# A linear-attention and channel-mix kernel: nine token slots per partition, two-row-group matmuls, and every engine in a fixed planned order

## The chip, the cores and the metric

One core of a Trainium2 chip runs the whole kernel. The metric is device time in microseconds (us), the median over executions. The core has five engines with a queue each: TensorE (PE in the profile, its weight loads PEld), VectorE (DVE), ScalarE (ACT), GpSimd (POOL) and SyncE (SP). DMAs are issued from POOL (those that also change the type from f32 to bf16) and from SP.

## The reference

For 8 batches, 8 heads, 576 tokens and head size 64:

```
proj = x @ w_phi                       # 64 -> 128, for x = q and x = k
proj = proj - max|proj| over features  # one number per token
phi  = [exp(proj), exp(-proj)]         # 256 features
kv = k_p^T v ; z = sum of k_p          # per head, over 576 tokens
attn = (q_p kv) / (q_p z + 1e-6)
x = attn, heads side by side           # (8, 576, 512)
xk, xr = token mixes of x and x one token earlier
out = sigmoid(xr @ w_r) * (relu(xk @ w_k)^2 @ w_v)   # 512 -> 1024 -> 512
```

Note that the maximum is subtracted before both exponentials: exp(p - m) and exp(-(p - m)).

## The kernel before, in words

**Pairs.** `attention_pair` (L144) handles two heads of one batch; there are 32 pairs. Head h keeps tokens 4p to 4p+3 on partition p (512 tokens), and the last 64 tokens of the two heads share one extra 128-partition group, the tail. DMA transposes (L137, SP) turn `nat` (tokens on partitions) into `qkT` (the 64 features of two token groups stacked on 128 partitions). One projection matmul multiplies such a block by `wboth`, two copies of w_phi on the diagonal of a 128x256 matrix of which half is zero.

**The k maximum** is not subtracted in the projection. DVE takes max|proj| (L161, L163), ACT makes exp(-m) and exp(+m) (`em`, L171, L172), and POOL multiplies v by them into `v12` (L178, L181), two versions of v that kv (L231) reads. **The q maximum** is transposed through TensorE (`mhl`, L197 to L200, copied out at L202) and added to the transposed q projection by small matmuls with the selector `sel` (L212).

**The mix and the channel mix.** `mix` (L274) builds xk and xr for a whole batch on DVE (L284 to L295) after its four pairs. `moe` (L298) runs 32 matmuls for h (L304), ReLU on ACT (L307), a square on POOL (L308), 16 matmuls for r (L313), 32 for v (L319), and a last DVE step (L322). Tails of two batches are joined into one smaller `moe` call.

**Order.** Python issues the four pairs of batch b and then the channel mix of batch b-1 (L336 to L349). The framework's scheduler orders each engine's queue by itself and weaves the two. PSUM has 8 banks: tag P (2 buffers of 2 banks: ps_k, ps_q, ps_qT), tag B (2 of 1 bank), tag mo (2 of 1 bank). Each engine runs its queue in order: an instruction that waits holds up what stands behind it.

Of the kernel before, what the change touches and what calls it, by code (L numbers as in the profile page):

```python
# [8 lines left out]
FP = mybir.dt.float32  # L9
# [3 lines left out]
AX = mybir.AxisListType  # L13


@with_exitstack
def kernel(
# [15 lines left out]

    nc = tc.nc
# [6 lines left out]
    SM = 512  # L41
    TAIL = S - SM
    NDC = DM // 128
    NFC = FF // 128
    NG = 9 * NP
    XW = 128 + S
# [3 lines left out]
    mid = ctx.enter_context(tc.tile_pool(name="mid", bufs=3))  # L50
    small = ctx.enter_context(tc.tile_pool(name="small", bufs=4))
    xpool = ctx.enter_context(tc.tile_pool(name="xpool", bufs=2))
# [15 lines left out]
    nc.gpsimd.tensor_copy(ident, ident_f32)

    sel2 = consts.tile([128, 9], FP, name="sel2")  # L70
    nc.vector.tensor_tensor(sel2, ident_f32[:, 0:9], ident_f32[:, 9:18], op=ALU.add)
    sel = consts.tile([128, 9, 128], BF, name="sel")
    nc.vector.tensor_copy(sel, sel2.to_broadcast([128, 9, 128]))
    hmask = consts.tile([128, 2], FP, name="hmask")
    nc.vector.memset(hmask, 0.0)
    nc.vector.memset(hmask[0:64, 0:1], 1.0)
    nc.vector.memset(hmask[64:128, 1:2], 1.0)

    NMH = 3
    mhls = []  # L80
    for i in range(NMH):
        t = consts.tile([128, 128], BF, name=f"mhl{i}")
        nc.vector.memset(t, 0.0)
        mhls.append(t)
    NVT = 2
    vts = []
    for i in range(NVT):
        t = consts.tile([128, H, 5, D], FP, name=f"vt{i}")
        nc.gpsimd.memset(t[:, :, 4, :], 0.0)
        vts.append(t)  # L90

# [6 lines left out]
    def load_weights():  # L98
        nc.sync.dma_start(out=mu_k_t, in_=moe_mu_k.rearrange("(c p) -> p c", p=128))
        nc.sync.dma_start(out=mu_r_t, in_=moe_mu_r.rearrange("(c p) -> p c", p=128))  # L100
        nc.gpsimd.dma_start(out=wk_bf, in_=moe_w_k.rearrange("(c p) f -> p c f", p=128))
        nc.gpsimd.dma_start(out=wr_bf, in_=moe_w_r.rearrange("(c p) f -> p c f", p=128))
        nc.gpsimd.dma_start(out=wv_bf, in_=moe_w_v.rearrange("(c p) f -> p c f", p=128))
        nc.vector.tensor_scalar(wv_bf, wv_bf, 0.5, None, op0=ALU.mult)

    def load(b, parts):
        nat = inp.tile([128, NG, 128], BF, name="nat")
        qkT = inp.tile([128, NG, 128], BF, name="qkT")  # L110
        vt = vts[b % NVT]
        flat = nat.rearrange("p g c -> p (g c)")
        flatT = qkT
        tails = flat[:, 32 * 128:].rearrange("p (a t d) -> p a t d", a=NP, t=2)
        for (a0, a1) in parts:
            hs = slice(2 * a0, 2 * a1)
            for (src, base) in ((k, 16), (q, 0)):
                nc.gpsimd.dma_start(
                    out=flat[:, (base + 4 * a0) * 128:(base + 4 * a1) * 128].rearrange(
                        "p (h x) -> p h x", x=256),  # L120
                    in_=src[b, hs, 0:SM, :].rearrange("h (p j) d -> p h (j d)", j=4))
            for (src, t) in ((k, 1), (q, 0)):
                for hh in range(2):
                    nc.gpsimd.dma_start(  # L124
                        out=tails[64 * hh:64 * hh + 64, a0:a1, t, :],
                        in_=src[b, 2 * a0 + hh:2 * a1:2, SM:S, :].rearrange("a i d -> i a d"))
            nc.sync.dma_start(
                out=vt[:, hs, 0:4, :].rearrange("p h j d -> p h (j d)"),
                in_=v[b, hs, 0:SM, :].rearrange("h (p j) d -> p h (j d)", j=4))
            for hh in range(2):  # L130
                nc.sync.dma_start(
                    out=vt[64 * hh:64 * hh + 64, 2 * a0 + hh:2 * a1:2, 4, :],
                    in_=v[b, 2 * a0 + hh:2 * a1:2, SM:S, :].rearrange("a i d -> i a d"))
            rng = [(0, NG)] if (a0, a1) == (0, NP) else [
                (16 + 4 * a0, 16 + 4 * a1), (4 * a0, 4 * a1), (32 + a0, 32 + a1)]
            for (g0, g1) in rng:
                nc.sync.dma_start_transpose(out=flatT[:, g0:g1, :],  # L137
                                            in_=flat[:, g0 * 128:g1 * 128])
        return qkT, vt

    xs_of = {}
    pair_no = [0]

    def attention_pair(b, hp, qkT, vt):  # L144
        n = pair_no[0]
        pair_no[0] += 1
        xs = xs_of[b]
        gq, gk, gt = 4 * hp, 16 + 4 * hp, 32 + hp


        ps_k = psum.tile([128, 8, 128], FP, name="ps_k", tag="P", bufs=2)
        for g in range(4):
            nc.tensor.matmul(ps_k[:, 2 * g:2 * g + 2, :].rearrange("p c f -> p (c f)"),  # L153
                             lhsT=qkT[:, gk + g, :], rhs=wboth,
                             start=(g % 2 == 0), stop=(g % 2 == 1))

        ps_t = psum.tile([128, 4, 128], FP, name="ps_t", tag="B", bufs=2)
        nc.tensor.matmul(ps_t[:, 0:2, :].rearrange("p c f -> p (c f)"),
                         lhsT=qkT[:, gt, :], rhs=wboth, start=True, stop=True)
# [12 lines left out]
        nc.scalar.activation(em[:, 1, :], mkf, AF.Exp)  # L172
        emt = em.rearrange("p a (h j) -> p a h j", h=2)[:, :, :, 4]
# [206 lines left out]
```

## Time and profile before

| | |
|---|---|
| median of 2 runs | 507.23 us (506.62 to 507.83) |
| the profiled execution, its own time | 509.07 us |
| its span in the trace | 507.3 us |
| mean granted TensorE clock | 0.942 |
| DMA traffic | 40.92 MB |

The span is what the trace covers from the first to the last instruction. Busy time is the time in which an engine executes; matmul ends are modelled. "Idle before" is time for which an engine stood still just before an instruction, with the one that released it.

### The profile page before, as it was taken

What the parts mean: (1) busy time and instruction counts of PE and PEld (TensorE: products, weight loads), DVE (VectorE), ACT (ScalarE), POOL (GpSimd) and SP (SyncE); (2) the same over time, 40 slices, a digit from 0 to 9 for tenths busy, and PEclk for the clock granted to TensorE, in tenths of its full rate; (3) what the DMA queues carried; (4) which work ended last, traced back from release to release, by engine and by line L of the source; (5) the groups of instructions that cost most, each with busy time, mean ns of one, the idle gap of its engine ahead of it and who ended that gap; (6) DMA issues with size and microseconds to landing.
All of it is one profiled execution on the core that took longest, in us unless ns stands there. A gap on an engine that the chain in (4) does not pass through costs nothing.

```text
span 507.3 us, 7519 instructions
## 1 busy us (share of the span) xinstructions
PE 336.2 (66%) x2832; PEld 194.5 (38%) x2832; DVE 296.2 (58%) x615; ACT 213.2 (42%) x389; POOL 247.1 (49%) x374
## 2 busy tenths in 40 slices
PE   0131434566875868877875688768857887888695
PEld 0011223343443434544443445435434554445232
DVE  1031403467845795686568755875567659874921
ACT  1020313243643454556444554476344734753232
POOL 8534152246643465377327753574237426662342
PEclk9999999999898799989997899899958998889899
DMA  9999980178018800990149404600460011001012
GB/s 153 181 196 191 143 95 0 60 128 95 0 43 229 94 1 21 209 156 1 43 129 150 45 22 146 124 3 22 129 121 0 22 43 43 1 1 63 21 42 63
DMA packets 84515, 40.92 MB, mean 81 GB/s; under 512 B 53120, under 2 KB 79360, under 8 KB 84480
## 3 DMA queue, kind: packets, MB, share of 16 engines
q1 hardware_dynamic: 56752, 28.39, 24.2%
q0 software_dynamic: 27728, 12.06, 19.9%
q8 instruction: 22, 0.36, 0.3%
q14 instruction: 13, 0.11, 0.1%
HBM read 33.62 MB, written 9.44 MB: 85 GB/s over the span
## 4 chain that ended last, share of the span: by engine, by line
PE 31%; POOL 30%; DVE 18%; DMA 10%; issue 7%; ACT 4%; POOLq 0%; DVEq 0%; ACTq 0%
POOL v L178 15%; PE ps_v L319 6%; POOL kk L308 6%; DMA nat<-in_q_dram 5%; PE ps_h L304 5%; DMA qkT<-nat 4%; PE ps_kv L231 4%; PE ps_r L313 3%; DVE xr L290 3%; PE ps_nd L249 3%; DVE mk L161 2%; PE ps_k L153 2%; DVE tr L293 2%; POOL nat L124 2%; DVE x_sc L260 2%
## 5 line engine op out<-in xcount | busy, mean ns | idle before, releaser
L308 POOL TENSOR_TENSOR kk<-krelu 128x512 bf16<-128x512 bf16 (+1 forms) x96 | 85.1, 904 | 90.7 <-ACT krelu L307 90.2
L178 POOL TENSOR_TENSOR v<-vt,em 128x640 bf16<-128x640 f32 x64 | 82.6, 1314 | 1.1
L304 PE MATMUL ps_h<-xk,wk_bf 128*128 128x512 bf16 x256 | 77.2, 420 | 6.6 <-DVE xk L290 4.9
L319 PE MATMUL ps_v<-wv_bf,kk 128*128 128x512 bf16 x288 | 75.5, 379 | 1.4 <-POOL kk L308 1.4
L307 ACT ACTIVATE krelu<-ps_h 128x512 bf16<-128x512 f32 (+1 forms) x96 | 46.2, 497 | 70.8 <-PE ps_h L304 61.6
L223 ACT ACTIVATE q_p<-ps_qT 128x1024 bf16<-128x1024 f32 x32 | 32.8, 1026 | 97.1 <-PE ps_qT L212 97.0
L185 ACT ACTIVATE k_p<-ps_k 128x1024 bf16<-128x1024 f32 x32 | 32.8, 1024 | 66.7 <-DVE mk L161 66.7
L231 PE MATMUL ps_kv<-v,k_p 128*128 128x65 bf16 x256 | 16.4, 209 | 58.4 <-POOL v L181 55.9
L161 DVE TENSOR_REDUCE mk<-ps_k 128x8 f32<-128x1024 f32 x32 | 39.1, 1221 | 24.6 <-PE ps_k L153 24.4
L236 DVE CAST kv<-ps_kv 128x260 bf16<-128x260 f32 x32 | 13.7, 427 | 60.7 <-PE ps_kv L233 60.6
L197 POOL CAST mhl<-nm 128x9 bf16<-128x9 f32 x32 | 9.5, 298 | 78.7 <-DVE nm L166 78.7
L304 PEld LDWEIGHTS <-wk_bf 128*128 128x128 bf16 x384 | 34.8, 103 | 33.7 <-issue 14.5
L194 DVE TENSOR_REDUCE nm<-ps_q 128x8 f32<-128x1024 f32 x32 | 39.0, 1218 | 14.2 <-PE ps_q L191 14.1
L322 DVE SCALAR_TENSOR_TENSOR ob<-rt,ps_v 128x512 f32<-128x512 bf16 x36 | 24.7, 686 | 30.2 <-PE ps_v L319 18.4
L316 ACT ACTIVATE rt<-ps_r 128x512 bf16<-128x512 f32 x36 | 21.7, 602 | 44.4 <-PE ps_r L313 43.9
L153 PE MATMUL ps_k<-wph,qkT 128*128 128x256 bf16 x128 | 23.8, 306 | 23.9 <-DMA qkT<-nat 22.5
L207 PE MATMUL ps_qT<-qkT,wph 128*128 128x512 bf16 x64 | 29.3, 458 | 11.2 <-DVE nm L194 10.4
L319 PEld LDWEIGHTS <-kk 128*128 128x128 bf16 x288 | 26.4, 98 | 25.1 <-POOL kk L308 2.6
L313 PE MATMUL ps_r<-wr_bf,xr 128*128 128x512 bf16 x128 | 35.6, 379 | 0.0
L290 DVE SCALAR_TENSOR_TENSOR xr<-diff,mu_r_t,xs 128x512 bf16<-128x512 bf16 x32 | 34.8, 1088 | 0.0
L224 ACT ACTIVATE q_n<-ps_qT 128x1024 bf16<-128x1024 f32 x32 | 33.4, 1044 | 0.0
L191 PE MATMUL ps_q<-wph,qkT 128*128 128x256 bf16 x128 | 26.7, 320 | 9.6 <-ACT k_n L186 9.1
(81 smaller groups left out, 696.7 us busy)
## 6 DMA issues: line engine op xcount, KB each, us to landing
out_dram<-ob SPq DMA_DIRECT2D x32, 256.0 KB, 2.4
vt<-in_v_dram SPq DMA_DIRECT2D x7, 1024.0 KB, 6.5
nat<-in_k_dram POOLq DMA_DIRECT2D x7, 512.0 KB, 6.4
nat<-in_q_dram POOLq DMA_DIRECT2D x7, 512.0 KB, 8.9
vt<-in_v_dram SPq DMA_DIRECT2D x4, 256.0 KB, 4.7
wk_bf<-in_moe_w_k_dram POOLq DMA_DIRECT2D x1, 1024.0 KB, 9.0
wv_bf<-in_moe_w_v_dram POOLq DMA_DIRECT2D x1, 1024.0 KB, 17.6
out_dram<-ob SPq DMA_DIRECT2D x8, 128.0 KB, 2.7
```

What stands on the lines that cost most here:

```text
L153: nc.tensor.matmul(ps_k[:, 2 * g:2 * g + 2, :].rearrange("p c f -> p (c f)"), lhsT=qkT[:, gk + g, :], rhs=wboth, start=(g % 2 == 0), stop= ...
L161: nc.vector.tensor_reduce(mk[:, :, 0:4], ps_k.rearrange("p (h j) f -> p h j f", h=2), axis=AX.X, op=ALU.max, apply_absolute_value=True)
L178: nc.gpsimd.tensor_tensor(v12[:, pn, :, 0:64], vp.rearrange("p (s d) -> p s d", d=D), em[:, pn, :].to_broadcast([128, 10, D]), op=ALU.mult)
L194: nc.vector.tensor_reduce(nm[:, 0:8], ps_q, axis=AX.X, op=ALU.max, apply_absolute_value=True, negate=True)
L224: nc.scalar.activation(q_n, qT8, AF.Exp, scale=-1.0)
L231: nc.tensor.matmul(ps_kv[:, pn, h, :], lhsT=kx[:, c, :], rhs=v12[:, pn, 5 * h + j, :], start=(pn == 0 and c == 0), stop=False)
L290: nc.vector.scalar_tensor_tensor(out=xo[:, c, :], in0=diff[:, c, 0:SM], scalar=mu[:, c:c + 1], in1=xs[:, c, 0:512], op0=ALU.mult, op1=ALU.add)
L304: nc.tensor.matmul(ps_h[:, 0:w], lhsT=wk_bf[:, c, fc * 128:(fc + 1) * 128], rhs=xk[:, c, :], start=(c == 0), stop=(c == NDC - 1))
L307: nc.scalar.activation(krelu[:, 0:w], ps_h[:, 0:w], AF.Relu)
L308: nc.gpsimd.tensor_tensor(kk[:, fc, 0:w], krelu[:, 0:w], krelu[:, 0:w], op=ALU.mult)
L313: nc.tensor.matmul(ps_r, lhsT=xr[:, c, cs], rhs=wr_bf[:, c, :], start=(c == 0), stop=(c == NDC - 1))
L319: nc.tensor.matmul(ps_v, lhsT=kk[:, fc, cs], rhs=wv_bf[:, fc, :], start=(fc == 0), stop=(fc == NFC - 1))
```

## The change

It rewrites the kernel's body.

- **Layout.** Token = 9p + s with 64 partitions per head; two heads fill 128 partitions, nine slots s each, no tail tokens. Per pair k has slots 0 to 8 and q slots 0 to 8, which give nine transposed blocks: four of k, four of q, and one ("edge") that holds slot 8 of k on rows 0 to 63 and slot 0 of q on rows 64 to 127. One edge block per pair is handled for four pairs at once (`add_edge`). Loads are one DMA each for k, q and v per batch (batch 0 in three parts).
- **Row-tiled matmuls.** Projections, maximum adds and kv use 64 of the 128 rows of the array per matmul, in pairs on rows 0 to 63 and 64 to 127 that write different PSUM banks. The zero halves of `wboth` go.
- **The k maximum** goes the way of the q maximum: both are negated, transposed together, and `ka` adds the k one to the finished projection in PSUM. v is only cast to bf16 (`vc`); exp(m), exp(-m) and `v12` go.
- **Moved work.** The kv copy goes from DVE to ACT. The mix is made per pair (`df`, `xa`, `xb`). The two divisions per pair become one pass of 640 columns.
- **PSUM.** Tag P has 3 buffers of 2 banks, mo 2 of 1 bank, B goes.
- **Order.** Every step is registered with an engine, a cost, a due time (one pair each T = 8.2) and the buffers that it takes and frees; `Plan.order` places them greedily, the engine that can start soonest first, and the code is emitted in that order under a manual schedule. In the plan a `nat` buffer counts as free when SP has issued the transposes that read it (cost 0.6 on SP), and the next load into it stands on POOL from then on; on the chip that load waits for the transposes themselves.

```diff
+LAG = {"PE": 0.25, "ACT": 0.2, "DVE": 0.15, "POOL": 0.2, "SP": 0.05, "DMA": 1.8}
+SWITCH = 0.12
+    def order(self, bufs, loose=()):
...
+                if e == "PE":
+                    cands = [(t + (SWITCH if o["mode"] != self.mode else 0.0), o) for (t, o) in cands]
+                t0 = min(c[0] for c in cands)
+                pick = min((c for c in cands if c[0] <= t0 + 0.12),
+                           key=lambda c: (c[1]["due"], c[1]["idx"]))
+                if best is None or pick[0] < best[0]:
+                    best = pick
...
+        op(f"lk{tag}", "POOL", 0.7, due, ld(0), alloc=al("nat"), chain="lk")
+        op(f"lq{tag}", "POOL", 0.7, due, ld(1), [f"lk{tag}"])
+        op(f"tr{tag}", "SP", 0.6, due, tr, [f"lk{tag}.d", f"lq{tag}.d"], alloc=al("qkT"),
+           rel=[("nat", b)])
+        op(f"tr{tag}.d", "DMA", 1.5 * n, due, None, [f"tr{tag}"])
...
+    for i, (nm_, dst, src, g) in enumerate((("wk", wk_bf, moe_w_k, 6.5), ("wr", wr_bf, moe_w_r, 3.2),
+                                            ("wv", wv_bf, moe_w_v, 6.5))):
+        op(nm_, "POOL", 0.7, i - 8, ldw(dst, src), ["tr1.0"])
...
+        def proj(tag, gg):
+            ps = ptile(("P", tag + N), "ps_" + tag)
+            for g in range(4):
+                for par in range(2):
+                    r = slice(64 * par, 64 * par + 64)
+                    nc.tensor.matmul(ps[:, par, g * 128:(g + 1) * 128],
+                                     lhsT=qkT[b][r, g0 + gg + g, :], rhs=wph[r, :],
+                                     start=(g == 0), stop=(g == 3))
...
+        def ka():
+            for par in range(2):
+                r = slice(64 * par, 64 * par + 64)
+                nc.tensor.matmul(s["k"][:, par, :], lhsT=s["mT"][r, :],
+                                 rhs=sel[r, 0:4, :].rearrange("p g f -> p (g f)"),
+                                 start=False, stop=True, skip_group_check=True)
...
+        def kv():
+            s["kvp"] = ps = ptile(("P", "kv" + N), "ps_kv")
+            for pn in range(2):
+                for c in range(8):
+                    par, g = divmod(c, 4)
+                    for hh in range(2):
+                        r = slice(64 * hh, 64 * hh + 64)
+                        nc.tensor.matmul(ps[:, hh, pn * 65:(pn + 1) * 65], lhsT=s[f"k{pn}"][r, c, :],
+                                         rhs=vb[r, a, 2 * g + par, :],
+                                         start=(pn == 0 and c == 0), stop=False)
...
+        op("qp" + N, "PE", 0.25, d0, qp, [f"tr{pt}.d", "dve1"], alloc=[("P", ("P", "q" + N))], chain="qp",
+           mode=1, rel=[("qkT", b)])
...
+        op("mh" + N, "POOL", 0.5, d0 + 2, mhx, ["rk" + N, "dve2"], alloc=al("mhl"), rel=[("nm", n)],
+           chain="mh")
+        op("mt" + N, "PE", 0.06, d0 + 2.2, mt, ["mh" + N, "dve3"], rel=[("mhl", n)],
...
+        op("kv" + N, "PE", 0.65, d0 + 6, kv, ["eb" + N, "vc" + N, f"ekt{pt}"],
...
+        op("kc" + N, "ACT", 0.4, d0 + 6.5, kvc, ["kv" + N], rel=[("P", "kv" + N)], alloc=al("kvs"),
```

Per pair the steps are, in this order of need: `qp`, `kp` (projections, 8 matmuls of 128 columns each), `rq`, `rk` (maxima, DVE), `mh` (POOL), `mt` (transpose), `mc` (DVE), `ka` (2 matmuls of 512), `qt` (2 of 512 and 8 of 128), `ea`, `eb`, `qa`, `qb` (exponentials of 1024 columns, ACT), `kv` (36 matmuls of 65), `kc`, `nd` (18, full array), `rd` (DVE), `xt` (5 transposes), `xe`, `df`, `xa`, `xb` (DVE). The channel mix keeps its matmuls, with 128 edge tokens from each two batches (`add_moe_edge`).

## Rows read from the trace of the kernel before

**Rows 1.** The page, busy time of each engine: us, share of the span, instructions.

```profile
PE 336.2 (66%) x2832; PEld 194.5 (38%) x2832; DVE 296.2 (58%) x615; ACT 213.2 (42%) x389; POOL 247.1 (49%) x374
```

**Rows 2.** Windows: from:to, length, busy us (instructions) of each engine, clock, DMA share, GB/s.

```profile
20.00:40.00 20.00, 5.32 (x19) 2.48 (x20) 5.52 (x6) 4.18 (x6) 8.03 (x13) 1.00 1.28 188
40.00:60.00 20.00, 7.28 (x62) 5.20 (x62) 5.72 (x14) 4.74 (x8) 7.09 (x10) 1.00 1.46 180
...
212.00:264.00 52.00, 40.84 (x368) 23.47 (x366) 35.41 (x71) 28.76 (x54) 29.05 (x46) 0.97 0.43 85
...
368.00:420.00 52.00, 39.17 (x353) 23.52 (x353) 34.53 (x76) 26.20 (x49) 24.06 (x36) 0.87 0.21 49
```

**Rows 3.** Chain that ended last, 200 to 264 us: start, us, engine, tile, line.

```profile
208.04 8.00 DMA qkT<-nat
...
236.07 2.48 POOL v L178 x2
...
246.94 2.44 POOL v L178 x2
```

**Rows 4.** Waits: who waited for whom, total us, times, longest us.

```profile
PE ps_kv L231 <- POOL v L181: 55.9, 26, 13.3
...
POOL nat L118 <- DMA qkT<-nat: 25.0, 4, 11.9
```

**Rows 5.** Chain, 200 to 264 us: TensorE groups at full clock, us and count.

```profile
205.63 0.26 PE ps_kv L231 x8
...
206.59 0.52 PE ps_nd L249 x16
...
250.30 0.22 PE ps_qT L212 x4
...
250.83 0.22 PE ps_qT L207
251.04 0.86 PE ps_r L313 x4
```

**Rows 6.** Timeline, TensorE: start, duration, of one nd matmul.

```profile
155.19 0.19 PE L249 MATMUL ps_nd<-kv,q_n 128*128 128x65 bf16 x1
```

**Rows 7.** Lines, shapes apart: busy us, mean ns, idle before and its releaser.

```profile
L178 POOL TENSOR_TENSOR v<-vt,em 128x640 bf16<-128x640 f32 x64 | 82.6, 1314 | 1.1
L308 POOL TENSOR_TENSOR kk<-krelu 128x512 bf16<-128x512 bf16 x64 | 70.9, 1123 | 68.7 <-ACT krelu L307 68.5
L161 DVE TENSOR_REDUCE mk<-ps_k 128x8 f32<-128x1024 f32 x32 | 39.1, 1221 | 24.6 <-PE ps_k L153 24.4
L307 ACT ACTIVATE krelu<-ps_h 128x512 bf16<-128x512 f32 x64 | 37.6, 607 | 56.9 <-PE ps_h L304 52.8 <-POOL kk L308 3.9
L290 DVE SCALAR_TENSOR_TENSOR xr<-diff,mu_r_t,xs 128x512 bf16<-128x512 bf16 x32 | 34.8, 1088 | 0.0
L223 ACT ACTIVATE q_p<-ps_qT 128x1024 bf16<-128x1024 f32 x32 | 32.8, 1026 | 97.1 <-PE ps_qT L212 97.0
L260 DVE TENSOR_TENSOR x_sc<-ps_nd,rden 128x320 bf16<-128x320 f32 x64 | 31.1, 488 | 1.4
L322 DVE SCALAR_TENSOR_TENSOR ob<-rt,ps_v 128x512 f32<-128x512 bf16 x36 | 24.7, 686 | 30.2 <-PE ps_v L319 18.4 <-issue 7.7 <-ACT t_n L221 3.5
L267 DVE COPY xs<-ps_x 128x512 bf16<-128x512 bf16 x32 | 13.4, 419 | 3.4 <-PE ps_x L265 3.3
```

**Rows 8.** Timeline, VectorE: one mix step with POOL idle beside it.

```profile
228.20 0.74 DVE L290 SCALAR_TENSOR_TENSOR xr<-diff,mu_r_t,xs 128x512 bf16<-128x512 bf16 x1
```

**Rows 9.** Windows around one long stop of TensorE, columns as in rows 2.

```profile
158.00:161.00 3.00, 0.10 (x1) 0.10 (x1) 3.00 (x5) 1.78 (x4) 0.71 (x3) 1.00 1.25 242
...
164.00:167.00 3.00, 2.29 (x20) 1.75 (x20) 1.74 (x4) 0.00 (x0) 2.14 (x6) 0.50 0.02 5
```

**Rows 10.** Chain, the end of the kernel: start, us, what.

```profile
472.03 0.49 DVE diff L285
...
478.31 9.71 POOL kk L308 x8
```

More of the change, by code (lines that the diff above doesn't have):

```diff
@@ L63 @@
-    wboth = wph.rearrange("p a f -> p (a f)")
+    BUFS = {"P": 3, "mo": 2, "nat": 2, "qkT": 2, "vt": 2, "v1": 2,
+            "kpn": 2, "qpn": 2, "tl": 2, "xk": 2, "kk": 2, "krelu": 3, "rt": 3, "ob": 3,
+            "xs": 2, "mhl": 3, "mk": 3, "nm": 3, "mT": 3, "kvs": 2, "x": 2, "me": 2, "d": 2, "mTe": 2}
+    T = 8.2
+    plan = Plan()
+    op = plan.op
+    wph_f32 = consts.tile([128, F], FP, name="wph_f32")
+    wph = consts.tile([128, F], BF, name="wph")
     ident_f32 = consts.tile([128, 128], FP, name="ident_f32")
-    make_identity(nc, ident_f32)
@@ L67 @@
     ident = consts.tile([128, 128], BF, name="ident")
[L68 to L90, printed above, removed]
+    sel3 = consts.tile([128, 3, 8], FP, name="sel3")
+    sel = consts.tile([128, 8, 128], BF, name="sel")
+    mhls = [consts.tile([128, 128], BF, name=f"mhl{i}") for i in range(BUFS["mhl"])]
@@ new lines, with get, heads @@
+    op("wphi", "SP", 1.2, -60, c_wphi)
+    op("wphi.d", "DMA", 0.1, -60, None, ["wphi"])
+    op("ident", "POOL", 1.5, -49.5, c_ident)
+    op("dve1", "DVE", 0.2, -9, c_dve1, ["wphi.d"])
+    op("dve2", "DVE", 0.6, -8, c_dve2)
+    op("dve3", "DVE", 0.8, -7, c_dve3, ["ident"])
+    nat, qkT, vt = {}, {}, {}
+    def get(dct, key, pool, shape, dtype, name, **kw):
+        if key not in dct:
+            dct[key] = pool.tile(shape, dtype, name=name, **kw)
+        return dct[key]
+    def heads(src, b, a0, a1):
+        return src[b, 2 * a0:2 * a1].rearrange("h (p s) d -> (h p) (s d)", s=R).rearrange(
+            "(a r) x -> r a x", r=128)
@@ new lines, in add_load, with ld, f, ldv @@
+    def add_load(b, a0, a1, due, first):
+        al = lambda t: [(t, (t, b))] if first else []
+        n = a1 - a0
+        tag = f"{b}.{a0}"
+        def ld(which):
+            def f():
+                t = get(nat, b, inp, [128, NP, 2 * X], BF, "nat")
+                src, o = ((k, 0), (q, X))[which]
+                nc.gpsimd.dma_start(out=t[:, a0:a1, o:o + X], in_=heads(src, b, a0, a1))
+            return f
+        def ldv():
+            t = get(vt, b, inp, [128, NP, X], FP, "vt")
+            nc.sync.dma_start(out=t[:, a0:a1, :], in_=heads(v, b, a0, a1))
+        def tr():
+            t = get(qkT, b, inp, [128, NP * R, 128], BF, "qkT")
+            nc.sync.dma_start_transpose(out=t[:, R * a0:R * a1, :],
+                                        in_=nat[b][:, a0:a1, :].rearrange("p a x -> p (a x)"))
+        g = 1.0 * n
+        op(f"lk{tag}", "POOL", 0.7, due, ld(0), alloc=al("nat"), chain="lk")
+        op(f"lk{tag}.d", "DMA", g, due, None, [f"lk{tag}"])
+        op(f"lq{tag}", "POOL", 0.7, due, ld(1), [f"lk{tag}"])
+        op(f"lq{tag}.d", "DMA", g, due, None, [f"lq{tag}"])
+        op(f"tr{tag}", "SP", 0.6, due, tr, [f"lk{tag}.d", f"lq{tag}.d"], alloc=al("qkT"),
+           rel=[("nat", b)])
+        op(f"tr{tag}.d", "DMA", 1.5 * n, due, None, [f"tr{tag}"])
+        op(f"lv{tag}", "SP", 0.6, due + 0.1, ldv, alloc=al("vt"), chain="lv")
+        op(f"lv{tag}.d", "DMA", g, due + 0.1, None, [f"lv{tag}"])
@@ L353 @@
+    BUFS["kke"] = 1
+    for b in range(B):
+        add_moe(b)
+        if b % 2 == 1:
+            add_moe_edge(b // 2)
+    seq = plan.order(BUFS, ("P", "mo"))
+    with tc.manual_schedule():
+        for o in seq:
+            if o["fn"] is not None:
+                o["fn"]()
 _INS = ['q', 'k', 'v', 'w_phi', 'moe_mu_k', 'moe_mu_r', 'moe_w_k', 'moe_w_v', 'moe_w_r']
```

754 lines of the change are left out of this document (521 added, 233 removed).

## The prediction

> **What bounds the kernel now.** I read the busy times first. No engine is busy for more than 66% of the span [rows 1], so no single engine sets the time. In a steady stretch of 52 us TensorE works 41 of them and VectorE 35 [rows 2]: about 13 us pass per pair. Next the chain of waits: it goes through POOL's two passes over v in every pair, 2.48 us at 236.07 and 2.44 us at 246.94 [rows 3]. The waits show why: kv waited for these passes 26 times, 55.9 us in all [rows 4]. So the kernel runs at the length of a chain, in which POOL's multiplication of v stands between the k maximum and kv. The change takes that multiplication out, so what is left is (a) the work of the busiest engine per pair and (b) what an order fixed in advance adds.
>
> **TensorE per pair afterwards.** Durations at full clock: 4 matmuls of 512 columns take 0.86 us, 4 of 128 take 0.22, 8 of 65 take 0.26, one of 512 takes 0.22 [rows 5].
> - Channel mix: 80 matmuls of 512 per batch, 20 x 0.86 = 17.2; edge tokens 32 of 128 and 12 of 512 per two batches, (1.76 + 2.58) / 2 = 2.2. Sum 19.4 per batch, 4.84 per pair. Nothing is saved here.
> - Full-array attention: nd 0.52 [rows 5] and two matmuls of 130 columns (0.12 by columns), five transposes 0.28, mt 0.06: 0.98.
> - Row-tiled: if the two halves of the array run one after the other, qp 0.44, kp 0.44, ka 0.44, qt 0.88, kv 36 x 0.0325 = 1.17, edge block 0.29: 3.66. If they run side by side, half, 1.83. No row shows two matmuls side by side; I take the middle, 2.75, and keep both ends.
>
> The Trainium skill (TensorE: Matmul & The Clock Gate, Measured speedup vs the span model) gives 3.07x for four row tiles of 512 columns. The same efficiency with two tiles would be 1.54x, an estimate from that page, and by it the term would be 2.4; no run here shows it.
> - Changes between whole-array and row-tiled matmuls, about 10 per pair, each between nothing and the tail of one matmul: 0.19 duration [rows 6] less a pitch of 0.03 [rows 5] is 0.16. So 0 to 1.6. Matmuls of different shapes follow each other without a gap (250.83 + 0.22 against 251.04 [rows 5]), which is the nearer row, so I take a fifth, 0.3.
> - Clock: the granted clock is 0.97 in one stretch of 52 us and 0.87 in another [rows 2]. I take 0.95.
>
> (4.84 + 0.98 + 2.75 + 0.3) / 0.95 = **9.3 us per pair**.
>
> **The other engines per pair.** ACT: four exponentials 4 x 1.03, kv copy about 0.45 (a copy of 512 took 0.42), two ReLUs and a tanh 3 x 0.61, edges 0.6, edge tokens of the channel mix 0.2 [rows 7]: 7.2. POOL: the cast of v at most 1.2 (1.31 for 640 columns), 2.25 squares x 1.12, small ones 0.6, DMA issue 0.4 [rows 7]: 4.7; before, the two v passes alone were 2.6. VectorE: two maxima 2.44, edge maximum 0.31, division 0.98, copies of x about 1.0, ob 1.125 x 0.69 = 0.77 [rows 7], a difference 0.49 [rows 10], small ones 0.4, and two mix steps of 576 columns. One of 512 columns takes 0.74 with POOL idle [rows 8] and 1.09 in the mean [rows 7], so 1.7 to 2.45: VectorE has 8.1 to 8.8. So TensorE leads, with VectorE close behind; a kv copy moved to ACT costs nothing while ACT keeps 2 us of room. The removed em, v12 and tail steps were work on ACT, POOL and DVE and give time only through the chain.
>
> **The start.** Each batch moves 3.5 MB (k and q as bf16 1.2, v 1.2, transposed copy 1.2, by their sizes). Two batches, 7.1 MB, at the 180 to 188 GB/s of the first 60 us [rows 2], with 2 us before the first issue, take 41 us; batch 2's k and q (1.2 MB) get in between, 6 more. The first pair starts when its own third is there, but POOL's load of batch 3 waits in its queue for batch 1's transposes, and every `mh` behind it waits as well. So I take 48 us at which three pairs are through (40 to 55).
>
> **A wait that the change adds.** The plan frees `nat` 0.65 after the transposes are issued; on the chip POOL's next load must wait until they have read it. A batch's transposes took 8.00 us [rows 3], and such waits are there already, 4 of them with 25.0 us [rows 4]. With VectorE and TensorE pacing, POOL is idle half the time, so it reaches that load within about 1 us; behind it stand `mh` (so mt, ka, kv), the squares (so v) and the casts. TensorE has only what is already released. That is about 6 us for each of batches 4 to 7: 24 in all, 0 to 44, the upper end with 8 us each and 3 more for the clock: after 3 us with TensorE at 0.10 busy the granted clock fell to 0.50 [rows 9], the lower level of 1.2 GHz.
>
> **The end.** From the last batch's mix to the end of the span it is 507.3 - 472.03 = 35.3 us, of which 6.3 pass until the first square [rows 10]. The mix is now made pair by pair, so about 5 go: 30.
>
> **Sum.** 48 + 29 x 9.3 + 24 + 30 = 372 us of span. The profiled execution took 509.07 with a span of 507.3, 1.8 more, and the median, 507.23, lies 1.8 below it; the two cancel, and **372 us** stands for the runs.
>
> **Rivals.**
> - *The plan holds.* Row tiles run side by side (7.65 / 0.97 = 7.9), so VectorE sets 8.1 per pair, and POOL's loads land beside stretches in which TensorE has released work. 45 + 29 x 8.1 + 30 = **310 us**. For: POOL, which the chain now waits for, gets room. Against: VectorE's mix steps stretch beside POOL [rows 7, 8]. The Trainium skill (SBUF — State Buffer, Who interferes with whom) has a VectorE instruction with two SBUF inputs block against a GpSimd one that reads SBUF; by that rule, with which 1.09 against 0.74 agrees, every mix step keeps this exposure and the case would reach 8.8 per pair, 330. Chance 0.22.
> - *Row tiles give nothing.* The halves run one after the other and each change of shape drains the array: (4.84 + 0.98 + 3.66 + 1.6) / 0.95 = 11.7 per pair, 48 + 29 x 11.7 + 24 + 30 = **441 us**. For: single matmuls last 0.19 against a pitch of 0.03, so a drain has that much to lose. Against: before, groups of different shape run without a gap. The Trainium skill (TensorEngine Tiling (Array Packing), Key Properties) says that changing the tiling mode drains TensorE; that is this case's half, and no row here shows it. Chance 0.21.
> - *Slower: the fixed order ties the pairs together.* If the next pair's qp and kp stand behind this pair's kv in the order, for want of one of three P buffers, a pair takes its chain: two maxima 2.44, mh and mt about 0.8, mc 0.2, four exponentials 4.1 [rows 7], the TensorE groups qp, kp, ka, qt, kv, nd 4.0, copy 0.45, division 1.2, transposes and copies of x 1.3, about 14.5, and one channel-mix unit of 0.86 in front: 15.4. Then 48 + 29 x 15.4 + 24 + 30 = **549 us**. It decides from (507 - 102) / 29 = 14.0 per pair. Against: buffer hold times sum to some 16 us per pair over three buffers, 5.5 per pair, and the plan prices them. Chance 0.05.
>
> **Numbers.** Forecast 0.50 (own range 340 to 405, from 8.4 to 10 per pair and the bounds on the start and on POOL's waits), 0.22, 0.21, 0.05, and 0.02 for a middle of no change. From 305 to 445 the range leaves out some 0.08 of the plan's case, 0.07 above the third, and the slow one. A measurement of this kernel tells about 2% from no change. Faster by over 2%: 0.93; within: 0.02; slower: 0.05.
>
> **What would show it.** POOL's load of k idle before by 4 to 8 us on DMA qkT, with mt behind it; qp of 8 matmuls in 0.25 to 0.45 us and kv in 0.6 to 1.2; VectorE at 80 to 90% and TensorE ahead of it in steady stretches; mix steps near 1.2 us; first maxima near 16 us and three pairs at 48; v passes gone from the chain. The prediction is wrong if pairs take 8.1 or less, if 11 or more, or if POOL does not wait on the transposes.

## The result and the profile after

The changed kernel takes **413.66 us** (413.09 to 414.23, 2 runs) against 507.23: ratio 0.8155, 95% interval 0.8092 to 0.8219. That is clearly faster, but 42 us above the forecast of 372 and outside the forecast's own range of 340 to 405. Runs of one and the same kernel can fall into a faster and a slower state, more than 1.5% apart: medians and ranges below hold all runs, ratios those of the faster state. The profiled execution took 413.09 with a span of 411.3 and a mean granted clock of 0.942, the same clock as before.

The busy times on the page (us, share of the span, instructions), to be held against [rows 1]:

```profile
PE 307.0 (75%) x3712; PEld 169.8 (41%) x3758; DVE 254.1 (62%) x456; ACT 209.6 (51%) x309; POOL 137.5 (33%) x237
```

POOL fell from 247.1 to 137.5 us, TensorE from 336.2 to 307.0 and VectorE from 296.2 to 254.1. Still no engine is busy for more than three quarters of the span.

The waits (who waited for whom: us in all, times, longest), against [rows 4]:

```profile
POOL kk L650 <- ACT krelu L643: 98.8, 33, 13.5
POOL mhl L454 <- DVE nm L430: 69.7, 23, 9.3
...
POOL nat L256 <- DMA qkT<-nat: 43.7, 5, 11.0
...
PE ps_m L459 <- POOL mhl L455: 21.7, 7, 9.5
```

The wait of kv for POOL's v passes (55.9 us) is gone. The wait of POOL's load for the transposes has grown from 25.0 to 43.7 us. Seven times TensorE's `mt` (L459) waits for `mh` on POOL, up to 9.5 us. One such place, on POOL and on TensorE (start, duration, in brackets what was idle before and its releaser):

```profile
202.49 0.80 POOL L256 DMA_DIRECT2D nat<-in_k_dram  x1 [10.43 <-DMA qkT<-nat]
203.29 0.75 POOL L256 DMA_DIRECT2D nat<-in_q_dram  x1
204.02 2.12 POOL L439 CAST v<-vt 128x576 bf16<-128x576 f32 x3
206.10 0.71 POOL L454 CAST mhl<-nm 128x16 bf16<-128x16 f32 x1
206.90 0.67 POOL L455 TENSOR_TENSOR mhl<-nm,mhl 128x16 bf16<-128x16 f32 x1
```

```profile
202.84 0.39 PE L418 MATMUL ps_k<-wph,qkT 64*128 64x128 bf16 x8
207.63 0.29 PE L459 MATMUL ps_m<-ident,mhl 128*128 128x128 bf16 x1 [4.40 <-POOL mhl L455]
```

POOL stands 10.43 us at the load of k; behind it three v casts and `mh` have piled up, and TensorE stops for 4.40 us until `mh` has come. This is the wait that the prediction described. The clock pays for it too (columns as in [rows 2]; the stop, then the time behind it):

```profile
203.20:207.60 4.40, 0.02 (x2) 0.00 (x0) 4.21 (x7) 0.00 (x0) 4.31 (x8) 0.91 0.90 132
207.60:213.40 5.80, 4.87 (x12) 1.68 (x13) 2.49 (x3) 0.60 (x1) 0.99 (x3) 0.50 1.13 306
```

After 4.40 us in which TensorE did next to nothing it worked for 5.8 us at a granted clock of 0.50, the lower level of 1.2 GHz.

The windows, columns as in [rows 2]: first eight pairs with two stops of POOL at its loads (the one above, and one of 9.11 us up to 163.8 behind which no `mt` of TensorE waited), then eight pairs without one, then five stretches of 10 us out of the latter.

```profile
144.30:237.30 93.00, 75.59 (x927) 41.47 (x939) 64.63 (x111) 51.87 (x75) 33.35 (x55) 0.91 0.48 103
237.30:321.80 84.50, 70.15 (x926) 39.20 (x937) 62.68 (x111) 51.78 (x76) 28.90 (x51) 0.99 0.30 58
247.00:257.00 10.00, 9.86 (x118) 5.22 (x119) 6.08 (x14) 6.31 (x10) 3.33 (x8) 1.00 0.77 146
257.00:267.00 10.00, 9.87 (x145) 5.48 (x143) 5.64 (x13) 6.16 (x8) 1.04 (x1) 1.00 0.50 108
267.00:277.00 10.00, 7.83 (x83) 3.78 (x78) 9.78 (x16) 5.19 (x10) 4.75 (x6) 1.00 0.00 0
277.00:287.00 10.00, 7.70 (x146) 4.69 (x146) 5.86 (x12) 9.13 (x15) 5.98 (x12) 1.00 0.11 20
307.00:317.00 10.00, 6.55 (x67) 3.42 (x69) 9.77 (x19) 4.43 (x8) 5.24 (x10) 1.00 0.01 2
```

Undisturbed, eight pairs take 84.5 us, **10.56 per pair**, at a clock of 0.99. The forecast was 9.3 at 0.95. TensorE works 70.15 of the 84.5 us, VectorE 62.68. In 247 to 267 TensorE is full, in 267 to 277 and 307 to 317 VectorE is, in 277 to 287 ScalarE nearly: full stretches take turns, and while one engine is full the others partly stand.

The end of the chain that ended last (start, us, what), against [rows 10]:

```profile
385.28 1.89 PE ps_h L636 x8
387.16 0.91 PE ps_r L657 x4
388.07 2.63 PE ps_h L636 x12
```

The last copy of x ends at 382.4 and the span at 411.3: 28.9 us, nearly all TensorE.

### The profile page after: what moved, and what is told of

Its sections match the earlier page's. It is cut to its first block, busy times and chain, and to the rows that moved or that the text cites. A ratio compares the mean times of both kernels' runs of the same rounds, so it can differ in the third digit from the quotient of the medians.

```text
span 411.3 us, 8965 instructions
## 1 busy us (share of the span) xinstructions
PE 307.0 (75%) x3712; PEld 169.8 (41%) x3758; DVE 254.1 (62%) x456; ACT 209.6 (51%) x309; POOL 137.5 (33%) x237
## 5 line engine op out<-in xcount | busy, mean ns | idle before, releaser
L650 POOL TENSOR_TENSOR kk<-krelu 128x512 bf16<-128x512 bf16 x64 | 67.1, 1062 | 98.9 <-ACT krelu L643 98.8
L445 ACT ACTIVATE k<-ps_k 128x1024 bf16<-128x1024 f32 x64 | 62.3, 1029 | 47.5 <-PE ps_k L468 33.5
L489 ACT ACTIVATE q<-ps_qT 128x1024 bf16<-128x1024 f32 x64 | 62.3, 1036 | 5.3 <-PE ps_qT L482 5.2
L643 ACT ACTIVATE krelu<-ps_h 128x512 bf16<-128x512 f32 x64 | 38.3, 613 | 45.6 <-PE ps_h L636 40.0
L430 DVE TENSOR_REDUCE nm<-ps_k 128x8 f32<-128x1024 f32 x32 | 39.0, 1218 | 4.6 <-PE ps_k L418 4.5
L566 DVE SCALAR_TENSOR_TENSOR xr<-diff,mu_r_t,xs 128x576 bf16<-128x576 bf16 x32 | 33.5, 1046 | 0.0
L566 DVE SCALAR_TENSOR_TENSOR xk<-diff,mu_k_t,xs 128x576 bf16<-128x576 bf16 x32 | 28.9, 903 | 1.1
L537 DVE TENSOR_TENSOR x_sc<-ps_nd,rden 128x640 bf16<-128x640 f32 x32 | 26.4, 824 | 1.1
L504 PE MATMUL ps_kv<-v,k 64*128 64x65 bf16 x1024 | 25.4, 202 | 2.0 <-ACT k L445 1.7
L504 PEld LDWEIGHTS <-k 64*128 64x128 bf16 x1024 | 22.6, 102 | 9.6 <-issue 6.8
L459 PE MATMUL ps_m<-ident,mhl 128*128 128x128 bf16 x32 | 7.6, 238 | 24.0 <-POOL mhl L455 21.7
```

What stands on the lines that cost most here:

```text
L430: nc.vector.tensor_reduce(s["nm"][:, 0, :], s["k"].rearrange("p a (g f) -> p (a g) f", f=128), axis=AX.X, op=ALU.max, apply_absolute_value ...
L445: nc.scalar.activation(s[f"k{pn}"], s["k"].rearrange("p a (g f) -> p (a g) f", f=128), AF.Exp, scale=(1.0 if pn == 0 else -1.0))
L489: nc.scalar.activation(t.rearrange("f h (c p) -> f c h p", c=8), s["qT"].rearrange("f a (g h p) -> f (a g) h p", g=4, h=2), AF.Exp, scale= ...
L504: nc.tensor.matmul(ps[:, hh, pn * 65:(pn + 1) * 65], lhsT=s[f"k{pn}"][r, c, :], rhs=vb[r, a, 2 * g + par, :], start=(pn == 0 and c == 0), ...
L537: nc.vector.tensor_tensor(s["x"].rearrange("p (b s) d -> p b s d", b=2), ndv[:, :, :, 0:64], s["rd"].to_broadcast([128, 2, 5, 64]), op=ALU ...
L566: nc.vector.scalar_tensor_tensor(out=t[:, a, (b % 2) * S:(b % 2 + 1) * S], in0=s["d"], scalar=mu[:, a:a + 1], in1=xs[:, a, 0:S], op0=ALU.m ...
```

## Experiments

All times are medians; "ratio" is against the kernel before in the same batch of runs, with its 95% interval. The changed kernel itself has 413.66 and 0.8155 (0.8092 to 0.8219). The kernels were timed in several batches, so both columns are given; where they differ the ratio is the fairer one.

| kernel | median (range) | ratio (interval) |
|---|---|---|
| loads of k and q later | 394.21 (391.46 to 396.08) | 0.7849 (0.7729 to 0.7968) |
| row halves one after the other | 415.06 (411.30 to 416.82) | 0.8258 (0.8139 to 0.8377) |
| half of the v matmuls | 399.44 (398.06 to 400.61) | 0.7965 (0.7863 to 0.8067) |
| framework's order | 401.39 (400.95 to 402.55) | 0.8000 (0.7926 to 0.8073) |
| second mix step out | 394.19 (392.00 to 397.60) | 0.7805 (0.7735 to 0.7876) |
| kernel before, v only cast | 453.39 (451.08 to 453.70) | 0.8961 (0.8897 to 0.9025) |
| framework's order, loads later | 401.12 (399.20 to 404.92) | 0.7950 (0.7863 to 0.8038) |
| loads later, difference on POOL | 388.47 (385.36 to 389.10) | 0.7674 (0.7612 to 0.7736) |
| second q exponential out | 413.05 (409.24 to 417.98) | 0.8153 (0.8038 to 0.8267) |
| 192 more tiling changes | 427.30 (419.96 to 429.37) | none given |
| loads later, difference on POOL, framework's order | 410.45 (405.05 to 414.25) | 0.8064 (0.7955 to 0.8174) |
| no maximum added to k | 412.67 (406.35 to 415.75) | 0.8159 (0.8073 to 0.8245) |

Two theories stood for the 42 us. **Theory 1:** POOL's loads, planned as if `nat` were free once the transposes are issued, stop POOL and with it `mh` and TensorE. **Theory 2:** the pace of the undisturbed pairs is not TensorE's sum, because in a fixed order several engines take turns at being the last. The rivals: row tiles do not overlap, tiling changes cost much, the planned order is at fault, the hand-offs on the way of the k maximum set the pace.

### 1. The loads of k and q later in POOL's queue

```diff
+    for b in range(3, B):
+        names = (f"lk{b}.0", f"lq{b}.0")
+        late = [o for o in seq if o["name"] in names]
+        seq = [o for o in seq if o["name"] not in names]
+        tr_t = min(o["t"] for o in seq if o["name"] == f"tr{b - 2}.0")
+        at = next(i for i, o in enumerate(seq) if o["t"] >= tr_t + 10.0)
+        seq[at:at] = late
```

> The changed kernel with one move: the loads of k and q of batches 3 to 7 stand later in POOL's queue, by 10 us of the plan, after the transposes that free their buffer. Every other queue is as in the changed kernel. Theory 1 (POOL's in-order wait on the transposes stops TensorE): the five waits of POOL on the transposes, 43.7 us, nearly go, and the time falls by 15 to 24 us, to 390 to 399. Two such waits lie in one stretch of eight pairs that took 92.9 us and none in the next, 84.5, so 4.2 us each. Rival (the waits are hidden, because TensorE has released work then): 409 to 414.

Measured: 394.21 us, 19.5 less than the changed kernel (0.031 of the ratio, 16 us). In its waits:

```profile
POOL nat L256 <- DMA qkT<-nat: 6.9, 3, 3.4
PE ps_m L459 <- POOL mhl L455: 3.5, 4, 1.4
```

So POOL's 43.7 us of waiting became 6.9, TensorE's 21.7 us of waiting for `mh` became 3.5, and 16 to 20 us of time went: theory 1 holds. The clock has a share in it: the mean granted clock rose from 0.942 to 0.965. Worked out from clock and span, the lower level costs 411.3 x 0.058 = 24 us of TensorE time in the changed kernel and 390.7 x 0.035 = 14 us here, so up to 10 us of the gain may have come through the clock (an estimate). Between the starts of the maxima of pairs 4 and 5 lay 22.3 us (45.2 to 67.5) in the changed kernel and 14.2 here; pairs 13 to 20 took 85.8 instead of 93.0. The pairs without a stop did not get faster (86.7 against 84.4, at a granted clock of 0.94 there against 0.99).

### 2. The row halves one after the other

```diff
-            for g in range(4):
-                for par in range(2):
+            for par in range(2):
+                for g in range(4):
...
-                for c in range(8):
-                    par, g = divmod(c, 4)
-                    for hh in range(2):
+                for hh in range(2):
+                    for c in range(8):
+                        par, g = divmod(c, 4)
```

> The changed kernel with the two row halves no longer alternating: in the projections, the q maximum adds and kv all matmuls of rows 0 to 63 come first and then all of rows 64 to 127, so that each half mostly runs alone. Same matmuls, same planned order. If the halves run side by side now and TensorE's queue is the pace, TensorE's work grows by about 0.2 + 0.2 + 0.2 + 0.5 = 1.1 to 1.4 us per pair and the time by 35 to 45, to 449 to 459. If TensorE has waits that take up part of it, 425 to 445. If the halves never ran side by side, 410 to 416.

Measured: 415.06 us, no difference that can be told. The timeline of TensorE says why the experiment did not take the overlap away from the projections. First this kernel, 8 of 128 columns and then kv:

```profile
129.74 0.41 PE L418 MATMUL ps_k<-wph,qkT 64*128 64x128 bf16 x8
129.98 0.45 PE L504 MATMUL ps_kv<-v,k 64*128 64x65 bf16 x13
130.25 0.20 PE L510 MATMUL ps_kv<-v,tk 64*128 64x65 bf16 x1
...
256.61 0.47 PE L504 MATMUL ps_kv<-v,k 64*128 64x65 bf16 x13
...
257.45 0.39 PE L671 MATMUL ps_v<-wv_bf,kk 128*128 128x512 bf16 x1
```

and the changed kernel:

```profile
202.60 0.40 PE L418 MATMUL ps_q<-wph,qkT 64*128 64x128 bf16 x8
...
249.71 0.42 PE L504 MATMUL ps_kv<-v,k 64*128 64x65 bf16 x16
249.96 0.20 PE L510 MATMUL ps_kv<-v,tk 64*128 64x65 bf16 x2
...
250.36 1.90 PE L671 MATMUL ps_v<-wv_bf,kk 128*128 128x512 bf16 x7
```

In both, eight projection matmuls of 128 columns take 0.24 us to the next group (202.60 to 202.84, 129.74 to 129.98), where four took 0.22 [rows 5]: two run at a time. kv with its 36 matmuls of 65 takes 0.65 us to the next group in the changed kernel (0.56 where no change of tiling follows) and 0.84 here. 32 pairs with 0.19 us more are 6 us of TensorE's work, and the kernel shows 1.4, inside its spread.

### 3. Every second v matmul left out

```diff
-                for fc in range(NFC):
+                for fc in range(0, NFC, 2):
```

> The changed kernel with every second of the eight matmuls of v in the main channel mix left out (that part of the sum is not computed): 4 x 4 x 0.216 = 3.5 us of TensorE less per batch, 28 in all, order unchanged. If TensorE's work sets the pace: 28 us less, 386. If waits at hand-offs between engines set it and TensorE's work lies partly beside them: 8 to 20 less, 394 to 406, of which 3.5 in the last batch. If another engine is the bound: 408 to 411.

It leaves out 128 matmuls of 512 columns, 128 x 0.22 = 28 us of TensorE. Measured: 399.44, 14.2 less by the medians and 10 by the ratios. Eight undisturbed pairs took 82.9 instead of 84.5. If TensorE's work alone set the pace, all 28 would have gone.

### 4. The framework's own order

```diff
-    with tc.manual_schedule():
+    if True:
```

> The changed kernel without the manual schedule: the same instructions, emitted in the planned order, but the framework's scheduler sets the order of each queue, as in the kernel before. Theory 1 (layout, row tiles and the k maximum in PSUM carry the gain, and the fixed order as such costs or gives little): 400 to 425. Rival (the planned order carries a large part of the gain): 430 to 490. If the framework's order avoids POOL's early waits on the transposes: 390 to 400.

Measured: 401.39, 12.3 less by the medians, 8 by the ratios: the planned order as it stands costs time. Its granted clock is 0.979 against 0.942; by the working of experiment 1 the clock takes 8 us of TensorE time from it and 24 from the changed kernel, which could be the whole gain. The framework's order waits less for the transposes (20.1 us against 43.7), and its undisturbed pairs run at the same pace (83.8 for eight):

```profile
POOL nat L256 <- DMA qkT<-nat: 20.1, 5, 5.9
```

### 5. The second mix step left out

```diff
+                if i == 1:
+                    return
...
-                    nc.tensor.matmul(ps, lhsT=xrt[bp][:, c, m0 + ci * 128:m0 + (ci + 1) * 128],
+                    nc.tensor.matmul(ps, lhsT=xkt[bp][:, c, m0 + ci * 128:m0 + (ci + 1) * 128],
```

> The changed kernel without VectorE's second mix step (xr is not computed; r reads xk instead): 33.5 us of VectorE less over the kernel, order unchanged. Theory 2 (after the start no engine sets the pace alone; stretches in which VectorE, TensorE and ScalarE are full take turns, so each engine's work counts for part): 10 to 22 us less, 392 to 404, as leaving out 28 us of TensorE's work gave 14. Rival (VectorE sets the pace): 30 us or more less, 384 or below. Rival (VectorE is hidden): 409 to 414.

It leaves out 32 mix steps, 33.5 us of VectorE (the r projection reads xk). Measured: 394.19, 19.5 less by the medians, 18 by the ratios: more than half of what was taken. So both TensorE's and VectorE's work counts, each in part, as theory 2 has it; the planned order, which theory 2 blames, is not tested by it.

### 6. The kernel before with v only cast

```diff
-        for pn in range(2):
-            nc.gpsimd.tensor_tensor(v12[:, pn, :, 0:64],
-                                    vp.rearrange("p (s d) -> p s d", d=D),
-                                    em[:, pn, :].to_broadcast([128, 10, D]), op=ALU.mult)
-        nc.gpsimd.tensor_copy(v12[:, :, :, 64], em)
+        nc.gpsimd.tensor_copy(v12[:, 0, :, 0:64], vp.rearrange("p (s d) -> p s d", d=D))
+        nc.gpsimd.memset(v12[:, 0, :, 64:65], 1.0)
```

> The kernel before with POOL's two multiplications of v replaced by one cast that does not depend on the k maximum, and em left out (v is not scaled, the maximum of k is not taken out): POOL, ACT and the chain k maximum - POOL - kv are relieved; layout, matmuls and order stay. If the gain of the change comes mainly from taking v's multiplication out of the chain: 440 to 465 (two passes of 1.24 us and 0.3 in each of 32 pairs are 89 us of POOL, 15% of the chain). If it comes mainly from the layout, the row tiles and the order: 485 to 505.

`em` goes too, so the k maximum is left out of v. Measured: 453.39, which is 53 of the 93.6 us that the change brought, 57%. It is the prediction's first statement, tested without the rest of the change (the two exponentials of `em` on ScalarE go with POOL's passes): the wait of kv for POOL's passes is gone from the list and POOL is down from 247.1 to 178.2:

```profile
PE 328.1 (73%) x2832; PEld 184.1 (41%) x2832; DVE 282.8 (63%) x615; ACT 203.4 (45%) x325; POOL 178.2 (40%) x310
```

The rest, some 40 us, comes from the other parts together; they were not taken apart.

### 7. The framework's order with the loads emitted later

The edit of experiment 1 (14 instead of 10 us behind the transposes) with that of experiment 4.

> The changed kernel in the framework's order (no manual schedule), with the loads of k and q of batches 3 to 7 emitted 14 us of the plan later. In the framework's order POOL's loads still waited 19 us in all on the transposes. If such a wait costs TensorE about half its length as before: 388 to 396, the fastest so far or even with the planned order with late loads (394). If the framework moves the loads early again: 399 to 403.

Measured: 401.12, as in experiment 4. POOL waited for the transposes 4 times, 19.0 us in all, and the load of batch 7 stood at 206.2 us, in experiment 4 at 206.7: the framework's order moved the loads forward again. So this says nothing new about theory 1.

### 8. Loads later, and the mix difference on POOL

The edit of experiment 1, and

```diff
-            nc.vector.tensor_tensor(s["d"], xs[:, a, 64:64 + S], xs[:, a, 0:S], op=ALU.subtract)
+            nc.gpsimd.tensor_tensor(s["d"], xs[:, a, 64:64 + S], xs[:, a, 0:S], op=ALU.subtract)
...
-        op("df" + N, "DVE", 0.4, d1 + 2, df, ["xe" + N], alloc=al("d"), chain="df")
+        op("df" + N, "POOL", 1.2, d1 + 2, df, ["xe" + N], alloc=al("d"), chain="df")
```

> The changed kernel with late loads and the difference of the mix moved from VectorE to POOL (18.8 us of VectorE, now some 35 of POOL, which is busy for a third of the span); the plan is made anew with that cost. Theory 2: VectorE's full stretches get shorter, 382 to 392 against 394 with late loads alone. Rival (POOL's added reading stretches VectorE's mix steps, and the hand-off lengthens the chain before h): 394 to 405.

Measured: **388.47**, the fastest of all and below both kernels (ratio 0.7674). Its interval touches that of experiment 1, so the move of the difference alone is not shown to help. On POOL a difference takes 1306 ns, on VectorE 588 ns in the changed kernel (line, tile, shapes, count, busy us, mean ns):

```profile
L560 POOL TENSOR_TENSOR diff<-xs 128x576 bf16<-128x576 bf16 x32 | 41.8, 1306 | 40.3 <-DVE xs L556 35.1 <-DVE xr L566 5.0
```

### 9. The second q exponential left out

```diff
+                if pn == 1:
+                    return
...
-                                     lhsT=s[f"q{pn}"][:, h, G * 128:(G + 1) * 128],
+                                     lhsT=s["q0"][:, h, G * 128:(G + 1) * 128],
```

> The changed kernel without the second exponential of q (exp of the negated projection is not computed; nd reads the first for both): 32 activations of 1.04 us, 33 us of ScalarE less and one step less in each pair's chain, order unchanged. Theory 2 (full stretches of TensorE, VectorE and ScalarE take turns): 8 to 22 us less, 392 to 406, as 28 us of TensorE gave 14 and 33.5 us of VectorE gave 19. If ScalarE, with 51% busy, is hidden: 409 to 414.

32 exponentials of 1.04 us go, 33 us of ScalarE (nd reads the first one twice). Measured: 413.05, no gain. ScalarE's work is covered in this order. Theory 2 is narrowed to TensorE and VectorE.

### 10. 192 more tiling changes

```diff
+                    if c == 1:
+                        nc.tensor.matmul(ps[:, 0:2], lhsT=zer[0:64, :], rhs=zer[0:64, 0:2],
+                                         start=False, stop=False, skip_group_check=True)
```

> The changed kernel with one matmul of 64 rows and 2 columns (zeros, added to the sum) in the middle of each of the 12 groups of four full-array matmuls for h and r per batch: 96 such, so 192 more changes between whole-array and row-tiled matmuls. If a change costs TensorE 0.10 to 0.12 us, as the gaps at such places show, TensorE has 19 to 23 us more in all; with half of it visible, as in the run with half of v's matmuls: 8 to 14 us more, 421 to 428. If changes were free and the gaps had another reason: 412 to 417. If a change costs a whole tail of 0.16 us: 430 or more.

One row-tiled matmul of two columns of zeros stands inside each of the 96 h and r groups of the full batches. Measured: 427.30 (419.96 to 429.37). The lowest run, which is the profiled one, lies 6 us above the changed kernel, between the two expectations; the other three lie together at 426.9 to 429.4 and are not taken as the price. The profile of that kernel shows what one pair of changes takes:

```profile
249.81 0.59 PE L661 MATMUL ps_r<-wr_bf,xr 128*128 128x512 bf16 x2 [0.69 <-ACT krelu L740]
250.34 0.17 PE L664 MATMUL ps_r<-zer 64*128 64x2 bf16 x1
250.44 0.60 PE L661 MATMUL ps_r<-wr_bf,xr 128*128 128x512 bf16 x2
```

Two matmuls of 512 take 0.43 us (half of 0.86 [rows 5]); the small one starts 0.53 after them and the next 0.10 after that: 0.20 for two changes. It is the same at 91 of the 96 places; at the other five the granted clock was 0.50 and it took longer. 96 x 0.20 = 19 us of TensorE's work, of which 6 appear in the profiled run. So a change costs TensorE 0.10 us; how much of that costs the kernel time is not settled.

### 11. Experiment 8 in the framework's order

> The kernel with the mix's difference on POOL and late loads, in the framework's order instead of the planned one. The framework's order took 401 with the difference on VectorE, and the move to POOL gave 6 us in the planned order: 390 to 399. If the framework's order, whose POOL loads still wait on the transposes, loses more with a busier POOL: 400 to 410. The planned order with the same two changes stands at 388.

Measured: 410.45, ratio 0.8064 against 0.7674 in the planned order. With the loads in their right place, the planned order is ahead. But the framework's order moves them: there POOL waits for the transposes 21.3 us in all, in experiment 8 5.6. So it does not set order against order alone; that the due place of ten loads is to blame, and not the planning, rests on experiment 1.

### 12. The maximum not added to k

```diff
-            for par in range(2):
+            for par in range(0):
```

> Part left out: the k maximum is not added to the projection in PSUM (the two ka matmuls per pair go), so the k exponentials wait for kp alone and ps_k is released without the way rk, mh, mt, mc, ka; all those other steps stay where they are in the order. Theory 2b, the hand-offs between engines on the way of the k maximum (which hold a P buffer for about 8 us of each pair) set the 10.56 us per pair: eight unstalled pairs fall from 84.5 to 78 or less and the kernel to 393 us or less. Theory 2a, TensorE and VectorE take turns at being full and this chain is covered: only the 7 us of TensorE matmuls go, of which half counts, 408 to 413 us. Rival, the k exponentials start earlier but stand in the same place in ScalarE's order, so nothing moves at all: 412 to 416 us.

The two `ka` matmuls per pair are left out, so the k exponentials wait for the projection alone. Measured: 412.67, ratio 0.8159. Two of the four runs are 4 and 7 us below the changed kernel and two are 2 above, so no more than the 7 us of matmuls that went can be seen; eight undisturbed pairs took 83.3. In them TensorE's waits for VectorE add up to 8.7 us (7.4 in the changed kernel): the waits of `ka` are gone and others stand in their place. The long hand-off of the k maximum (VectorE, POOL, TensorE, VectorE, TensorE) is covered by other work.

## Why the prediction was right, and where it failed

**Right: what bound the kernel before.** Experiment 6 takes POOL's multiplication out, with `em` and without the rest of the change, and gets 53 us.

**Right in kind, too large in size: the added wait.** The forecast was 24 us for the loads of batches 4 to 7; there were five stops (batches 3 to 7) of 5.0 to 11.0 us at POOL, and experiment 1 prices what they cost at 16 to 20. Of that, 8.1 us lie between pairs 4 and 5, at batch 3's load, which the prediction had put into its start; between pairs 5 and 21, where the loads of batches 4 to 7 stood, it is 11.4 (169.8 against 158.4), half of the 24. Only three of the five stops reached TensorE as a long wait of `mt`, of 9.51, 4.25 and 4.40 us, and two of these belong to batches 4 to 7; the other two stops held up no `mt`.

**Right: the end.** 28.9 us against 30.

**Failed: the step "so TensorE leads", with its 9.3 us per pair.** Measured: 10.56. The term was not too small; TensorE's own sum was even smaller than forecast. Row-tiled work is 1.83 instead of 2.75 (qp and kp 0.23 each, the 8 matmuls of qt, the 2 of qt and ka 0.22 each, kv 0.56, the edge block about 0.15): the halves run side by side, which was the lower end. Tiling changes: between a whole-array and a row-tiled matmul no gap was below 0.10 us, median 0.12 over 48 of them in 237 to 322, while groups of the same mode follow each other with a median gap of 0.003 us (97 places); six changes per pair instead of ten, about 0.65 instead of 0.3. The Trainium skill (TensorEngine Tiling (Array Packing), Key Properties) says that a change of mode drains TensorE; the trace agrees, at 0.10 to 0.12 us. So (4.84 + 0.98 + 1.83 + 0.65) / 0.99 = 8.4 us per pair, and the chip took 10.56. What failed is the use of the sum as the pace. That the forecast came as near as it did is partly luck: the row-tiled term, set too high, made up for some of it. With 8.4 its own sum gives 48 + 29 x 8.4 + 24 + 30 = 346.

What the runs put in its place: taking 28 us of TensorE's work gives 10 to 14, taking 33.5 of VectorE's gives 18 to 20, taking 33 of ScalarE's gives nothing, and taking out the k maximum's way at most its own matmuls. In the 84.5 us of the undisturbed stretch TensorE is busy for 70.15, 8.8 per pair. Its waits there add up to 7.4 us for VectorE, 4.8 for ScalarE and 0.9 for POOL; they are small and many, the longest groups being:

```profile
PE ps_k L468 <- DVE mT L463: 2.9, 3, 1.4
PE ps_x L545 <- DVE mT L463: 2.0, 1, 2.0
PE ps_e L355 <- DVE mTe L352: 1.0, 2, 0.7
PE ps_m L459 <- POOL mhl L455: 0.9, 1, 0.9
```

The first row is `ka` waiting for VectorE's copy `mc`, the second a transpose of x that is put down to the same copy. So the term that the prediction put at nothing is TensorE's waiting for the next engines, some 1.6 us per pair and most of it for VectorE, although VectorE is busy for only 74% there and not for the 80 to 90% foreseen. Experiments 3 and 5 bear it out in the same eight pairs: without `xr` TensorE's waits for VectorE fall from 7.4 to 2.3 us, with half of the v matmuls they rise to 9.8. In experiment 5 the granted clock in these pairs was 0.946 against 0.987, and TensorE was busy for 72.7 us instead of 70.15, which took part of the gain back. But no edit brought the pace of pairs 21 to 28 below 10.2 us (81.5 to 86.7 us for the eight, in the kernels where it was read), and what holds it there **stays open**. That it is the order planned in advance is not shown: the framework's own order has nearly the same pace (83.8). What the two share, queues that run in order and three P and two mo buffers, was not varied. Open is also why experiments 3 and 5 gained as much outside that stretch as they did: of the 16 us between the starts of pair 13 and pair 32 that experiment 5 saved, 2.9 lie in it.

**The sum again**, against the span of 411.3: forecast 48 + 29 x 9.3 + 24 + 30. Measured 29 x 10.56 = 306.2, POOL's stops 19.5 (by the medians), the end 28.9; what is left, 56.7, stands where 48 was. The errors: +36.5 from the pace, -4.5, -1.1, +8.7: 39.6 us of span. If batch 3's stop is counted into the start, as the prediction did, they are -12.6 for the stops and +16.8 for the start. The split holds for the sum and not place by place, because the pairs outside the undisturbed stretch had other paces: pairs 5 to 12, which meet less of the channel mix, took 76.8 us, and pairs 29 to 31 took 42.9. At the start the first maximum over a pair runs at 24.76, not near 16, because the first transposes keep the first projection waiting until 24.0; the fourth pair, at 45.2, was then close to the forecast of 48, but the fifth came 22.3 us later, POOL's first load wait and batch 1's transposes in between, of which experiment 1 takes 8.1 back.

**VectorE's mix steps** came out at 0.82 us alone and 1.60 beside POOL, with means of 0.90 and 1.05 (forecast near 1.2). VectorE and POOL at one place (start, duration):

```profile
268.19 0.81 DVE L566 SCALAR_TENSOR_TENSOR xr<-diff,mu_r_t,xs 128x576 bf16<-128x576 bf16 x1
...
274.36 1.60 DVE L566 SCALAR_TENSOR_TENSOR xr<-diff,mu_r_t,xs 128x576 bf16<-128x576 bf16 x1
```

```profile
274.05 1.30 POOL L650 TENSOR_TENSOR kk<-krelu 128x512 bf16<-128x512 bf16 x1 [1.11 <-ACT krelu L643]
```

The step that met POOL's square took twice as long. Of the 64 steps, the 39 with no POOL instruction beside them took 0.81 to 0.82 us each, the other 25 up to 1.63. The rule that the prediction weighed there (the Trainium skill, SBUF — State Buffer, Who interferes with whom) is in line with it.

**The rivals.** *The plan holds* (310) fell: its row tiles were there, but POOL's loads stopped the order and VectorE did not set 8.1. *Row tiles give nothing* (441) is nearer to the measured time than the forecast is, by 27 us against 42, but fell as a mechanism by the 0.24 us for eight matmuls; only its drain was real. *The fixed order ties the pairs together* (549) fell as a mechanism at that price: pairs overlap, and experiment 12 shows the chain of the k maximum covered. Its milder form is what was left out: a rival between 9.3 and 15.4 us per pair in which the engines wait for each other in turns and none runs full. The rows before offered it: TensorE busy 41 of 52 us [rows 2] with waits spread over many releasers is how this kernel looked already, and the forecast assumed that removing one chain would let one engine run full.

## What to carry to other kernels

A sum of the busiest engine's work is a lower bound for the pace, not the pace: when the next engine is close to it (here 7.8 us of VectorE beside 8.4 of TensorE) and each queue runs in order, expect full stretches to take turns, and price that (here 10.56). In a queue that runs in order, put a load whose buffer is still being read behind the work that others wait for; moving ten of them gave 16 to 20 us. Row-tiled pairs double the rate of small matmuls, but group them, because each change of tiling cost TensorE about 0.1 us here.

## What the runs showed of the hardware

- Two matmuls on rows 0 to 63 and 64 to 127 run at the same time: 8 of 128 columns in 0.24 us. They do so even when four of one half are issued before four of the other: in experiment 2 the eight starts of a projection come in pairs, 13 ns within a pair and 56 to 66 ns from pair to pair. Which half a start belongs to the trace does not say. But in that kernel's kv, where 16 matmuls are issued ahead of the first two edge ones (L510), only 13 had started when the first of these did: one half ran ahead of the order of issue. With these 36 small ones the overlap was partly lost (0.84 us against 0.65).
- A change between whole-array and row-tiled matmuls left a gap of at least 0.10 us in all 48 cases measured, against 0.003 between groups of the same mode, and two forced ones took 0.20 us at 91 of 96 places.
- After a stop of 4.40 us TensorE had a granted clock of 0.50 from 207.6 to 213.4 us, and with the stops gone its mean over the kernel rose from 0.942 to 0.965.
- A VectorE step with two SBUF inputs took 0.82 us with POOL idle and 1.60 us beside POOL's square of 1.30 us.
